# Attention's rows turned by VectorE's block transposes, and first weights in chunks of 128 rows

## The chip, the cores and the metric

The kernel runs on one core of one Trainium2 chip. The metric is the device time of one execution in microseconds (us). Before the change the median of 3 runs is 735.78 us (733.7 to 738.65).

## What is computed

Attention with two branches, then a layer of eight experts, of which each token takes one:

```python
# q, k, v: [8 batches, 8 heads, 576, 64] f32, about 0.1 x normal
q_d, k_d, v_d = means over each 4 tokens               # 144 tokens
out_up = repeat(softmax(q_d k_d^T / 8) v_d, 4)
scores = where(|i - j| < 4, q k^T / 8, -1e9)           # a band of 7 keys
attn_out = out_up + softmax(scores) v
x = attn_out.transpose(0, 2, 1, 3).reshape(4608, 512)  # column = 64 * head + d
logits = x @ w_gate + modality_bias[modality_id]       # w_gate [512, 8]
e = argmax(logits); gate = softmax(logits)[e]
out = gate * (relu(x @ w1[e]) @ w2[e])                 # w1 [8, 512, 1024], w2 [8, 1024, 512], all f32
```

## The kernel before

**Attention** works in 32 steps n, one for two heads of one batch (`b, hp = divmod(n, 4)`). A step loads q and k (L235) and v (L255) with SP's DMAs, turns q and k on TensorE (`tpq`, `tpk`, L279), copies them out of PSUM (`qT` on ScalarE, L299; `kT` on VectorE, L307), makes the band's scores (`sc`, L342), their maximum and exponentials, and turns the exponentials with VectorE's 32x32 block transposes (`lt`, L407). ScalarE spreads them into `Pw` (four copies, L412), and TensorE multiplies them with v (`avl`, L447). The branch of means goes through `scd` (L369), `de` (L382, L400), `pdt` (L418), `PdT` (L425) and `avd` (L432). VectorE adds both branches into X (L458). For a batch, X is `[128, 4, tokens]`: partition 64 a + d, second index 2 f + g, for the head 4 f + 2 a + g and its element d. GpSimd makes the sums over four (L313, L317) and two multiplications (L396, L400).

**Rows.** Each batch gives 4 or 5 tiles of 128 tokens, 36 in all. Per tile, `xr` turns X by four 128x128 transposes on TensorE into PSUM (L585; PSUM tag "T", of which there are three buffers, which q, k, the sums of v and `pdt` use too), `R` copies that on ScalarE into a row tile in the order of the reference's columns (L592), and `store` writes 128 rows of 2 KB to `xs` in HBM by one DMA of SP (L598). NR = 7 row tiles serve the first seven batches, four the last one.

**Routing.** Logits, the choice of expert and the places in a table are worked out for each batch (L494 to L575), and GpSimd scatters each token's number and gate into the table (L603). After four batches two units of 512 tokens are formed from the 2304 early rows; GpSimd fetches their table entries (L833) and gathers their rows from `xs` (L843).

**Experts.** 11 units follow: two early ones, six more of 512 tokens, one of 256, one of 128, one of 256. A unit needs an expert's weights in eight chunks of 512 KB: four of w1 (L792) and four of w2 (L795). A chunk lands in one of four `raw` buffers, ScalarE casts it to `hi` (L814) and VectorE subtracts for `lo` (L820); for the first four chunks GpSimd does part of that. There are 12 hi/lo buffers, used in turn; `step()` asks for a chunk four times in the first layer and four times in the second, eight chunks ahead. The gathered rows are turned on TensorE (L864) and split in the same way (L867, L869). Each product is three matmuls (hi x hi, hi x lo, lo x hi). A chunk of w1 holds all 512 rows and 256 of the 1024 columns, so `compute` needs chunk c for the output groups 2c and 2c+1 alone (L889). ReLU on ScalarE (L893) and VectorE (L894) gives the hidden values; the second layer (L937) goes to `o` (L940) and is scattered to the output by GpSimd (L941). The unit of 128 tokens (`compute_half`) has weights as the moving side, 256 columns at a time.

**Order.** Within Attention every instruction of every engine has a fixed place: `PHASE` gives each kind a due time in steps, `build` collects all calls, sorts them by `4 b + phase` or `n + phase`, and issues them in this order, so that each engine's queue is in the order of due times. SP's queue is one queue: the stores stand between the loads of q, k and v and, from the 28th step on, the first weights; a store that waits for its rows holds what is behind it. The last batch's routing and rows and the experts are ordered by a scheduler with priorities when the kernel is built.

Of the kernel before, what the change touches and what calls it, by code (L numbers as in the profile page):

```python
# [25 lines left out]
PAD = 3  # L26
# [19 lines left out]
NR = 7  # L46
# [33 lines left out]
class Consts:  # L80
# [48 lines left out]
    def load(s, tc, pool, work, rows, mid, bias, w_gate):  # L129
# [7 lines left out]
        s.mi = rows.tile([128, DM], F32, name="R", bufs=NR)[:36, :256].bitcast(I32)  # L137
# [41 lines left out]
    def biases(s, tc, pool, work, rows, psum):  # L179
# [11 lines left out]
        t1 = rows.tile([128, DM], F32, name="R", bufs=NR)[:, : 36 * NE].rearrange("p (t e) -> p t e", e=NE)  # L191
# [6 lines left out]
class Attention:  # L198
# [102 lines left out]
    def kT_(s, n, i):  # L301
# [4 lines left out]
        else:  # L306
            s.nc.vector.tensor_copy(s.kT2[:, g, PAD + 64 * g : PAD + 64 * g + 512], s.t.pop(("tp", "k", n)))  # L307
# [156 lines left out]
class Router:  # L464
# [116 lines left out]
    def xr(s, b, t):  # L581
        if t < s.t["G", b]:
            p = s.t["xr", b, t] = s.ps.tile([128, DM], F32, name="xr", tag="T", bufs=TB)
            for j in range(4):
                s.nc.tensor.transpose(p[:, 128 * j : 128 * j + 128], s.t["X", b][:, j, 128 * t : 128 * t + 128],  # L585
                                      s.C.ident)

    def R(s, b, t):

        if t < s.t["G", b]:  # L590
            R = s.t["R", b, t] = s.rp.tile([128, DM], F32, name="R", bufs=s.nr)
            s.nc.scalar.copy(R.rearrange("p (f a g d) -> p f g a d", f=2, a=2, g=2),  # L592
                             s.t.pop(("xr", b, t)).rearrange("p (f g a d) -> p f g a d", f=2, a=2, g=2))

    def store(s, b, t):
        if t < s.t["G", b]:
            r0 = 128 * (s.t["t0", b] + t)
            s.nc.sync.dma_start(s.xs[r0 : r0 + 128, :], s.t.pop(("R", b, t)))  # L598

# [625 lines left out]
```

## Time and profile before

| | us |
|---|---|
| median of 3 runs | 735.78 |
| the profiled execution's own time | 736.62 |
| its span, first to last instruction | 734.9 |
| Attention, up to the last `avl` matmul | about 288 |
| first expert matmul | 286.8 |
| last scatter to the output | 727.0 |

Times in the profile are us from the span's start. PE is TensorE's matmuls, PEld its weight loads, DVE VectorE, ACT ScalarE, POOL GpSimd, SP the engine that issues the plain DMAs. A line of a stage is `from:to length,` and then each engine's busy time with its count of instructions, the mean granted clock of TensorE, the mean busy share of 16 DMA engines, and GB/s. A group's line is: line, engine, operation, `out<-in`, shapes, count, then busy us, mean ns of one, idle time of the engine before it and what ended that. A wait's line is: who waited, for whom, total us, times, longest. A line of the timeline is start, length, engine, line, operation, count. "issue" is time in which an engine waited for nothing that the profile shows. Matmuls of TensorE overlap, so that a mean duration is longer than the distance between two.

### The profile page before, as it was taken

The numbers are of one execution on the slowest core, as the hardware profiler recorded it, in microseconds if no ns is written. First come the engines' busy times: TensorE is split into PE (matmuls) and PEld (weight loads), VectorE is DVE, ScalarE is ACT, GpSimd is POOL, SyncE is SP. The second block draws the span as 40 slices with busy tenths as digits, with TensorE's granted clock in tenths as the row PEclk, the third lists the DMA queues.
The fourth block names the chain that finished last, engine by engine and source line by source line (L and its number), as shares of the span: only waits on it lengthen the run. The fifth ranks groups of instructions, "written<-read, shape, count | busy, mean of one in ns | idle before, by whom it ended". The sixth has DMA issues, their size and how long they took to land. (4 is left out here: it accounts for less than half of the span.)

```text
span 734.9 us, 18972 instructions
## 1 busy us (share of the span) xinstructions
PE 682.7 (93%) x7635; PEld 555.0 (76%) x7635; DVE 379.5 (52%) x873; ACT 361.6 (49%) x808; POOL 298.7 (41%) x390
## 2 busy tenths in 40 slices
PE   6899898999968888997999999999999999999995
PEld 4678676777756766884888888888888888889894
DVE  4788575779745766650834424344243443326520
ACT  3578676777745766630434333343332433326620
POOL 6746564747757838266313243131412102211101
PEclk9899999999989999997999999999999999999998
DMA  9799999896786524944626235262452523526500
GB/s 180 154 192 176 184 187 182 159 211 119 172 156 195 86 85 113 278 146 154 200 74 217 86 118 194 82 219 72 143 172 96 191 85 99 175 87 211 180 13 28
DMA packets 175963, 107.89 MB, mean 147 GB/s; under 512 B 132765, under 2 KB 155329, under 8 KB 175874
## 3 DMA queue, kind: packets, MB, share of 16 engines
q1 hardware_dynamic: 167618, 87.44, 48.9%
q0 software_dynamic: 8256, 19.22, 7.9%
q8 instruction: 61, 1.00, 0.7%
q14 instruction: 28, 0.23, 0.1%
HBM read 87.39 MB, written 19.51 MB: 145 GB/s over the span
## 5 line engine op out<-in xcount | busy, mean ns | idle before, releaser
L820 DVE TENSOR_TENSOR wlo<-raw,whi 128x1024 fp32r<-128x1024 f32 x72 | 89.5, 1251 | 135.6 <-ACT whi L814 133.2
L941 POOL DMA_INDIRECT out_dram<-o,tg x37 | 39.6, 1070 | 253.6 <-ACT o L940 208.1
L814 ACT CAST whi<-raw 128x1024 fp32r<-128x1024 f32 x70 | 73.1, 1052 | 64.1 <-PE l L889 41.4
L937 PE MATMUL l<-whi,hh 128*128 128x512 f32 x256 | 100.5, 397 | 1.8 <-issue 1.7
L937 PE MATMUL l<-whi,hl 128*128 128x512 f32 x256 | 99.8, 392 | 1.1 <-issue 0.9
L937 PE MATMUL l<-wlo,hh 128*128 128x512 f32 x256 | 99.6, 391 | 1.1 <-issue 1.1
L889 PE MATMUL l<-xh,whi 128*128 128x512 f32 (+1 forms) x256 | 96.5, 379 | 0.6 <-issue 0.6
L889 PE MATMUL l<-xl,whi 128*128 128x512 f32 (+1 forms) x256 | 95.9, 375 | 0.8 <-issue 0.8
L889 PE MATMUL l<-xh,wlo 128*128 128x512 f32 (+1 forms) x256 | 96.0, 375 | 0.0
L940 ACT ACTIVATE o<-l,tg 128x512 f32<-128x512 f32 x37 | 25.4, 687 | 120.9 <-PE l L937 66.1
L893 ACT ACTIVATE hh<-l 128x512 fp32r<-128x512 f32 x72 | 42.8, 595 | 77.7 <-PE l L889 77.7
L894 DVE SCALAR_TENSOR_TENSOR hl<-l,hh 128x512 fp32r<-128x512 f32 x72 | 49.4, 688 | 59.8 <-ACT hh L893 59.8
L412 ACT COPY Pw<-lt 32x288 f32<-32x288 f32 x128 | 54.5, 426 | 7.8 <-DVE lt L407 6.1
L937 PEld LDWEIGHTS l<-whi,hl 128*128 128x128 f32 x256 | 48.2, 188 | 11.8 <-issue 2.5
L937 PEld LDWEIGHTS l<-wlo,hh 128*128 128x128 f32 x256 | 48.2, 188 | 11.6 <-issue 1.7
L937 PEld LDWEIGHTS l<-whi,hh 128*128 128x128 f32 x256 | 48.1, 188 | 11.3 <-issue 1.8
L889 PEld LDWEIGHTS l<-xl,whi 128*128 128x128 f32 x256 | 49.0, 191 | 9.8 <-issue 1.6
L889 PEld LDWEIGHTS l<-xh,whi 128*128 128x128 f32 x256 | 48.8, 191 | 9.6 <-issue 1.4
L889 PEld LDWEIGHTS l<-xh,wlo 128*128 128x128 f32 x256 | 48.8, 191 | 8.7 <-issue 0.4
L342 PE MATMUL sc<-kT,qT 64*24 64x32 f32 x3072 | 43.3, 193 | 10.9 <-issue 10.1
L603 POOL DMA_INDIRECT tab<-ig,si x36 | 39.1, 1086 | 34.4 <-DVE pn L720 12.2
L342 PEld LDWEIGHTS sc<-kT,qT 64*24 64x24 f32 x3072 | 33.7, 100 | 24.6 <-issue 20.2
(247 smaller groups left out, 1349.1 us busy)
## 6 DMA issues: line engine op xcount, KB each, us to landing
raw<-in_moe_w_dram SPq DMA_DIRECT2D x88, 512.0 KB
vw<-in_v_dram SPq DMA_DIRECT2D x53, 192.0 KB
xs<-R SPq DMA_DIRECT2D x36, 256.0 KB
qt<-in_q_dram SPq DMA_DIRECT2D x30, 288.0 KB
kt<-in_k_dram SPq DMA_DIRECT2D x30, 288.0 KB
vw<-in_v_dram SPq DMA_DIRECT2D x15, 96.0 KB
xg<-xs,tg POOLq DMA_INDIRECT x37
out_dram<-o,tg POOLq DMA_INDIRECT x37
```

The costliest lines, as they stand in the source:

```text
L342: s.nc.tensor.matmul(p[32 * j : 32 * j + SUB, i, :], qT[r, q0 : q0 + SUB], kT[r, q0 : q0 + WIN], start=False, stop=(i == NB - 1), skip_gro ...
L412: s.nc.scalar.copy(s.Pw[n % NPW][r, :, j, :SUB], s.t["lt", n][r, :, :SUB])
L603: i = nc.gpsimd.indirect_dma_start(out=s.tab[:, :], out_offset=bass.IndirectOffsetOnAxis(ap=C.si[:, t : t + 1], axis=0), in_=C.ig[:, t, :] ...
L814: (nc.gpsimd.tensor_copy if turn <= 4 else nc.scalar.copy)(hi, raw)
L820: (nc.gpsimd if 2 < turn <= 4 else nc.vector).tensor_tensor(lo, raw, hi.bitcast(F32), op=ALU.subtract)
L889: nc.tensor.matmul(p[:, 0 if H == 4 else f, :], a[:, k, fs], x[:, k, :N], start=(k == 0 and i == 0), stop=(k == 3 and i == 2))
L893: nc.scalar.activation(hh[:, g, :N], p, AF.Relu)
L894: nc.vector.scalar_tensor_tensor(hl[:, g, :N], p, 0.0, hh[:, g, :N].bitcast(F32), op0=ALU.max, op1=ALU.subtract)
L937: nc.tensor.matmul(p, a[:, f, hs], x[:, f % 2, :], start=(f == 0 and i == 0), stop=(f == 7 and i == 2))
L940: nc.scalar.mul(o, p, T[:, h, 1:2].bitcast(F32))
L941: nc.gpsimd.indirect_dma_start(out=s.out[:, :], out_offset=bass.IndirectOffsetOnAxis(ap=T[:, h, 0:1], axis=0), in_=o, in_offset=None, boun ...
```

## The change

1. `xr` and its PSUM tiles go. `R` is now a 32x32 block transpose on VectorE from X straight into the row tile. It turns each 32x32 block (32 partitions by 32 tokens), so a token's 512 values lie in four partition groups, in each as 4 x 32 values in a row. Two token tiles share a row tile of 4 KB a partition; NR = 4 of these serve the first batches, two the last one.
2. `store` writes two token tiles at a time (one, for the fifth of a batch) with four DMAs, one for each partition group, in pieces of 512 bytes. `xs` then has its 512 columns in another order: 16 groups of 32 values, sorted by partition group first.
3. So w1's rows are wanted in that order. A chunk of w1 is now 128 rows by all 1024 columns, loaded by four DMAs of 32 rows each (4 KB a row), and chunk k belongs to the k-th 128 values of a row. Every output group needs all four chunks. `compute` runs over output groups and then chunks; for the first unit, two output groups take chunks 0 and 1 and then chunks 2 and 3. `compute_half` multiplies 512 columns at a time.
4. `kT` is copied by ScalarE instead of VectorE, at another due time; R's due times stand where kT's had been within a step. The stores of a batch have three due times instead of five.

```diff
-NR = 7
+NR = 4
...
-    "tpq": 0.0000, "tpk": 0.0000, "qT0": 0.0000, "mk0": 0.0000, "tpt": 0.1888, "kT0": 0.2990, "qT1": 0.5097,
+    "tpq": 0.0000, "tpk": 0.0000, "qT0": 0.0000, "mk0": 0.0000, "tpt": 0.1888, "kT0": 0.2050, "qT1": 0.5097,
...
-    "X1": 3.6644, "X0": 3.6875, "xr0": 6.8416, "R0": 6.9346, "lg0": 7.0091, "lg1": 7.0155, "LT0": 7.1923,
-    "LT1": 7.2383, "xr3": 7.3162, "lgt0": 7.4172, "lgt1": 7.4353, "L1": 7.4440, "L0": 7.4639, "ch1": 7.4930,
-    "R3": 7.5485, "ch2": 7.5607, "ex": 7.6629, "gt": 7.8318, "pr": 7.8428, "xr4": 7.8664, "pl": 7.9316, "R4": 7.9883,
-    "xr1": 8.0166, "st4": 8.0780, "W0": 8.1749, "W3": 8.2403, "R1": 8.3185, "W4": 8.5513, "st2": 8.5946,
-    "st0": 8.7485, "xr2": 9.1244, "st3": 9.5946, "R2": 9.6525, "W1": 9.9527, "st1": 10.2000, "W2": 10.9537,
+    "X1": 3.6644, "X0": 3.6875, "lg0": 7.0091, "lg1": 7.0155, "LT0": 7.1923, "LT1": 7.2383, "R0": 7.2990,
+    "lgt0": 7.4172, "lgt1": 7.4353, "L1": 7.4440, "L0": 7.4639, "ch1": 7.4930, "ch2": 7.5607, "ex": 7.6629,
+    "R4": 7.7000, "gt": 7.8318, "pr": 7.8428, "pl": 7.9316, "st4": 8.0780, "W2": 8.1749, "R1": 8.2990, "W0": 8.5513,
+    "st2": 8.5946, "st0": 8.7485, "R2": 9.2990, "st3": 9.5946, "st1": 10.2000, "R3": 10.2990, "W1": 10.5513,
...
-            s.nc.vector.tensor_copy(s.kT2[:, g, PAD + 64 * g : PAD + 64 * g + 512], s.t.pop(("tp", "k", n)))
+            s.nc.scalar.copy(s.kT2[:, g, PAD + 64 * g : PAD + 64 * g + 512], s.t.pop(("tp", "k", n)))
...
-    def xr(s, b, t):
-        if t < s.t["G", b]:
-            p = s.t["xr", b, t] = s.ps.tile([128, DM], F32, name="xr", tag="T", bufs=TB)
-            for j in range(4):
-                s.nc.tensor.transpose(p[:, 128 * j : 128 * j + 128], s.t["X", b][:, j, 128 * t : 128 * t + 128],
-                                      s.C.ident)
-
     def R(s, b, t):
         if t < s.t["G", b]:
-            R = s.t["R", b, t] = s.rp.tile([128, DM], F32, name="R", bufs=s.nr)
-            s.nc.scalar.copy(R.rearrange("p (f a g d) -> p f g a d", f=2, a=2, g=2),
-                             s.t.pop(("xr", b, t)).rearrange("p (f g a d) -> p f g a d", f=2, a=2, g=2))
+            if t % 2 == 0:
+                one = t == 4 and b == B - 1
+                s.t["R", b, t // 2] = (s.rp.tile([128, 4, 4, 32], F32, name="o", bufs=3) if one else
+                                       s.rp.tile([128, 8, 4, 32], F32, name="R", bufs=s.nr))
+            R = s.t["R", b, t // 2][:, 4 * (t % 2) : 4 * (t % 2) + 4]
+            s.nc.vector.transpose(R, s.t["X", b][:, :, 128 * t : 128 * t + 128].rearrange("p k (i j) -> p i k j", j=32))
 
     def store(s, b, t):
-        if t < s.t["G", b]:
-            r0 = 128 * (s.t["t0", b] + t)
-            s.nc.sync.dma_start(s.xs[r0 : r0 + 128, :], s.t.pop(("R", b, t)))
+        n = min(2, s.t["G", b] - 2 * t)
+        if n > 0:
+            r0 = 128 * (s.t["t0", b] + 2 * t)
+            R = s.t.pop(("R", b, t))
+            for a in range(4):
+                s.nc.sync.dma_start(s.xs[r0 : r0 + 128 * n, 128 * a : 128 * a + 128].rearrange("(i j) x -> j i x", j=32),
+                                    R[32 * a : 32 * a + 32, : 4 * n].rearrange("p i k c -> p i (k c)"))
...
-            nc.sync.dma_start(raw.rearrange("p (k f) -> p k f", k=4),
-                              s.w1[bass.ds(e, 1), :, 256 * c : 256 * c + 256].rearrange("o (k p) f -> p (o k) f", p=128))
+            for i in range(4):
+                r = 256 * (i // 2) + 64 * (i % 2) + 128 * (c // 2) + 32 * (c % 2)
+                nc.sync.dma_start(raw[32 * i : 32 * i + 32], s.w1[bass.ds(e, 1), r : r + 32, :].rearrange("o p f -> (o p) f"))
...
+        early = H == 4 and s.turn["h"] == 0
+        for f, ks in [(f + j, k) for f in range(0, 8, 2) for k in ((0, 1), (2, 3)) for j in range(2)] if early else [
+                (f, range(4)) for f in range(8)]:
...
+            p, fs = ps[f // n], slice(128 * f, 128 * f + 128)
+            for k in ks:
+                wh, wl = W[k]
+                for i, (a, x) in enumerate(((wh, xh), (wh, xl), (wl, xh))):
+                    nc.tensor.matmul(p[:, f % n, :], a[:, fs], x[:, k, :N], start=(k == 0 and i == 0),
+                                     stop=(k == 3 and i == 2))
...
-            p = s.ps.tile([128, 2, 256], F32, name="l1", tag="S", bufs=SB)
-            for c in range(2):
-                step()
-                wh, wl = W[2 * g + c]
-                for k in range(4):
-                    for i, (a, x) in enumerate(((xh, wh), (xl, wh), (xh, wl))):
-                        nc.tensor.matmul(p[:, c, :], a[:, k, 0:128], x[:, k, :], start=(k == 0 and i == 0),
-                                         stop=(k == 3 and i == 2))
+            p = s.ps.tile([128, 512], F32, name="l1", tag="S", bufs=SB)
+            for k in range(4):
+                if k % 2 == 0:
+                    step()
+                wh, wl = W[k]
+                for i, (a, x) in enumerate(((xh, wh), (xl, wh), (xh, wl))):
+                    nc.tensor.matmul(p, a[:, k, 0:128], x[:, 512 * g : 512 * g + 512], start=(k == 0 and i == 0),
+                                     stop=(k == 3 and i == 2))
...
-            ro.rp, ro.nr = moe.xp, 4
+            ro.rp, ro.nr = moe.xp, 2
...
             for i in range(5):
-                ro.xr(b, i)
                 ro.R(b, i)
-                ro.store(b, i)
+                if i in (1, 3, 4):
+                    ro.store(b, i // 2)
```

More of the change, by code (lines that the diff above doesn't have):

```diff
@@ L136, in load @@
                                   w_gate[256 * f + 128 * a : 256 * f + 128 * a + 128].rearrange("(g d) e -> d g e", g=2))
-        s.mi = rows.tile([128, DM], F32, name="R", bufs=NR)[:36, :256].bitcast(I32)
+        s.mi = rows.tile([128, 2 * DM], F32, name="R", bufs=NR)[:36, :256].bitcast(I32)
         nc.sync.dma_start(s.mi, mid.bitcast(I32).rearrange("(t x) -> t x", t=36))
@@ L190, in biases @@
         s.tb = pool.tile([128, 36, NE], F32, name="tb")
-        t1 = rows.tile([128, DM], F32, name="R", bufs=NR)[:, : 36 * NE].rearrange("p (t e) -> p t e", e=NE)
+        t1 = rows.tile([128, 2 * DM], F32, name="R", bufs=NR)[:, : 36 * NE].rearrange("p (t e) -> p t e", e=NE)
         for dst, mm, r in ((s.tb, m0, 0), (t1, m1, 1)):
@@ L821, in wsplit @@
         if which == 0:
[L822 removed]
+            return hi, lo
         return hi.rearrange("p (f d) -> p f d", f=2), lo.rearrange("p (f d) -> p f d", f=2)
```

33 lines of the change are left out of this document (13 added, 20 removed).

## The prediction

> **What bounds the kernel now.** I read the page's head first, then busy time by stage, then groups of instructions, waits, and short stretches of the timeline. The page:
>
> ```profile
> span 734.9 us, 18972 instructions
> PE 682.7 (93%) x7635; PEld 555.0 (76%) x7635; DVE 379.5 (52%) x873; ACT 361.6 (49%) x808; POOL 298.7 (41%) x390
> ```
>
> TensorE is busy for 93% of the span, but that is a mean. By stage (busy us of each engine, clock, DMA share, GB/s):
>
> ```profile
> core 0: us, PE busy (x) PEld busy (x) DVE busy (x) ACT busy (x) POOL busy (x), PEclk, DMA share, GB/s
> 30.00:210.00 180.00, 168.32 (x3943) 133.40 (x3939) 133.93 (x417) 131.90 (x402) 114.35 (x164) 0.99 0.91 173
> 210.00:287.00 77.00, 59.73 (x1176) 47.95 (x1173) 46.68 (x133) 47.73 (x138) 50.44 (x63) 0.91 0.53 127
> 287.00:337.00 50.00, 50.00 (x261) 39.65 (x261) 28.07 (x79) 21.16 (x32) 27.41 (x24) 1.00 0.65 200
> 337.00:348.00 11.00, 5.62 (x12) 2.70 (x12) 0.00 (x0) 0.49 (x1) 5.99 (x6) 0.71 0.41 120
> 348.00:660.00 312.00, 312.00 (x1425) 258.50 (x1424) 126.68 (x162) 119.67 (x166) 73.94 (x70) 0.99 0.42 136
> 660.00:726.00 66.00, 64.85 (x401) 57.88 (x399) 27.59 (x29) 28.32 (x37) 6.20 (x6) 1.00 0.36 117
> ```
>
> Attention runs to 287 us. To 210 us TensorE is busy 168.3 of 180 us (94%), VectorE 74%, ScalarE 73%, and the DMA engines 91%: TensorE is the bound and DMA stands close behind. From 210 to 287 us TensorE has 17 us of holes. From 287 us the experts bind TensorE without a hole, but for 337 to 348 us. So work taken from TensorE is worth most of itself where its row is full, about half of itself from 210 to 287 us, and work given to VectorE or ScalarE is free unless their queues begin to bind.
>
> **What leaves TensorE.** The groups, and the transposes of Attention's rows by stage:
>
> ```profile
> L585 PE MATMUL xr<-ident,X 128*128 128x128 f32 x144 | 23.5, 289 | 0.1
> L592 ACT COPY R<-xr 128x512 f32<-128x512 f32 x36 | 20.8, 584 | 3.9 <-PE xr L585 3.6
> L307 DVE COPY kT<-tp 128x512 f32<-128x512 f32 x32 | 21.1, 658 | 10.1 <-PE tp L279 10.0
> L407 DVE STREAM_TRANSPOSE lt<-le 128x384 f32<-128x384 f32 x32 | 18.2, 569 | 8.9 <-POOL le L396 8.9
> L458 DVE TENSOR_TENSOR X<-avl,Od 128x288 f32<-128x288 f32 x48 | 20.3, 447 | 1.0 <-PE avl L447 0.8
> L458 DVE TENSOR_TENSOR X<-avl,Od 128x224 f32<-128x224 f32 x16 | 6.1, 380 | 0.2
> L299 ACT ACTIVATE qT<-tp 128x512 f32<-128x512 f32 x32 | 19.2, 600 | 10.7 <-PE tp L279 9.2 <-issue 0.6 <-ACT R L592 0.4
> 30.00:210.00 180.00, 13.77 (x88) 9.69 (x88) 12.84 (x22) 0.99 0.91 173
> 210.00:287.00 77.00, 6.92 (x36) 5.14 (x36) 5.26 (x9) 0.91 0.53 127
> 287.00:337.00 50.00, 2.83 (x20) 2.40 (x20) 2.71 (x5) 1.00 0.65 200
> ```
>
> 144 transposes are 36 tiles of four: 22 tiles to 210 us, 9 to 287 us, 5 among the first expert's matmuls. The busy time overstates them, since matmuls overlap. What a tile holds up is the distance to what starts next, in the timeline:
>
> ```profile
> 135.47 0.60 PE L279 MATMUL tp<-ident,qt 128*128 128x128 f32 x4
> 135.91 0.60 PE L279 MATMUL tp<-ident,kt 128*128 128x128 f32 x4
> 136.34 0.25 PE L333 MATMUL sc<-mask,identb 128*128 128x192 bf16 x1
> 136.43 0.60 PE L585 MATMUL xr<-ident,X 128*128 128x128 f32 x4
> 136.96 0.60 PE L342 MATMUL sc<-kT,qT 64*24 64x32 f32 x48
> ```
>
> Four transposes of this shape take 0.44 us (135.47 to 135.91). So 36 tiles give 15.8 us at most, as long as nothing else holds the end. That isn't all had:
>
> - The last 5 tiles stand between the first expert's matmuls, where TensorE has no hole: 5 x 0.44 = 2.2 us, all of it.
> - The 22 tiles before 210 us: 22 x 0.44 = 9.7 us. Here the other engines are near. One short step (of two heads) of the stage:
>
> ```profile
> 135.00:141.00 6.00, 6.00 (x163) 5.21 (x161) 5.12 (x14) 5.42 (x18) 5.56 (x9) 1.00 0.66 130
> ```
>
> ScalarE is busy 5.42 of 6.00 us, GpSimd 5.56. Such a step can shrink by 0.44 us, but only if every queue is entered without loss. I take 80%: 7.7 us. Bounds: 0, if ScalarE or GpSimd hold each step, and 9.7.
> - The 9 tiles of 210 to 287 us: 4.0 us, of which I take half, 2.0 us, since TensorE waits there for others a fifth of the time. Bounds 0 and 4.0.
>
> Together 11.9 us, bounds 2.2 and 15.8.
>
> **What VectorE and ScalarE get.** The new block transpose of 128x512 is not in the trace; its nearest row is the same operation on 128x384, 569 ns. By the two rows of L458, 64 elements more cost 67 ns, so 128 more cost 134 ns and the new one about 0.70 us. It reads X in four strided pieces; bounds are 0.57 us, and 1.14 us (two of the 384-wide). 36 of them are 25.3 us (20.5 to 41.0). VectorE gives up the 32 kT copies, 32 x 0.658 = 21.1 us, whose place in each step the transposes take. Net +4.2 us on an engine with 46 us idle before 210 us: 0. The Trainium skill, "VectorE: DVE Perf Modes", section "The three transpose paths", gives 311 ns for a 128x128 VectorE transpose in bf16; an estimate from that page is 4 x 311 = 1.24 us a tile, VectorE would gain 24 us of work and the sum would stay, with more weight on the second rival below. The row of 569 ns for three such blocks speaks against it.
>
> ScalarE loses 36 R copies, 21.0 us, and gets 32 kT copies from PSUM, priced as qT's at 600 ns: 19.2 us. Net -1.8 us: 0. But they move: the kT copy stands between qT and the three Pw copies for which TensorE's avl matmuls wait. Third rival.
>
> **Stores and queues.** SP's waits and issues (name of the issue: least, median, most ns), and the stretches that price a packet:
>
> ```profile
> SPq L795 <- DVE wlo L820: 158.9, 33, 19.3
> SPq L598 <- ACT R L592: 35.2, 12, 10.5
> SPq L235 <- PE tp L279: 15.0, 5, 6.4
> PE vp L267 <- DMA vw<-in_v_dram: 3.8, 2, 3.4
> L598 SPq DMA_DIRECT2D xs<-R x36: 319/584/3671, 76.1 to 311.2; - x36
> L792 SPq DMA_DIRECT2D raw<-in_moe_w_dram x44: 316/373/440, 229.9 to 679.9; - x44
> 30.00:60.00 30.00, 28.74 (x735) 23.10 (x732) 23.38 (x72) 22.88 (x74) 18.35 (x28) 1.00 0.92 181
> 327.00:331.00 4.00, 4.00 (x21) 3.27 (x21) 0.69 (x1) 1.16 (x2) 3.08 (x4) 1.00 0.90 311
> 690.00:695.00 5.00, 5.00 (x44) 4.92 (x42) 3.50 (x3) 3.50 (x5) 1.01 (x1) 1.00 0.93 309
> ```
>
> From 30 to 60 us nearly all is 256-byte loads of q, k and v: 181 GB/s at a share of 0.92 of 16 engines is 12.3 bytes per ns and engine, 21 ns a packet. From 327 to 331 us it is 1-KB pieces of the first weights: 21.6 bytes per ns, 47 ns. From 690 to 695 us it is mostly 2-KB pieces of the second: 20.8, so 99 ns. A 512-byte piece lies between 21 and 47 ns; on the line between them 30 ns. The stores are now 4608 packets of 2 KB, 28 us of 16 engines; they become 18432 of 512 bytes, 34 us (24 to 54). Over 230 us that is +6 us of DMA work. Loads of q, k and v have hidden nearly always: TensorE's largest wait for one is 3.8 us in all. SP itself waits 15.0 us for TensorE to free load buffers, so the loads run ahead. I take 0; without that cover it costs the 6 us.
>
> SP issues 80 store DMAs for 36, 44 more at 0.32 to 0.58 us: 14 to 26 us of SP; and four for one on 44 weight chunks, 132 more at 0.32 to 0.37 us: 42 to 49 us of SP over 490 us. SP waits 158.9 us for VectorE to free weight buffers on one line alone, so the weights have room. Behind a store that waits for R stand the loads of q, k and v; SP now waits at three places in a batch instead of four or five. 0.
>
> **First layer's order.** It does the same matmuls, but the first of a unit's eight output groups needs all four chunks. For the first unit the chunks are needed in pairs. Timeline of GpSimd and TensorE there:
>
> ```profile
> 288.37 2.38 POOL L820 TENSOR_TENSOR wlo<-raw,whi 128x1024 fp32r<-128x1024 f32 x1
> 286.78 0.96 PE L889 MATMUL l<-xh,whi 128*128 128x512 f32 x3
> 705.00:710.00 5.00, 5.00 (x44) 5.00 (x43) 0.69 (x1) 1.11 (x2) 0.97 (x1) 1.00 0.12 48
> ```
>
> The fourth chunk's low part ends at 290.75 us; it is wanted by the 18th matmul after 286.78 us, and with 0.22 us for one (312.0 us over 1425 from 348 to 660 us) that is 290.5 us. So 0 to 0.5 us; I take 0. The unit of one block has 24 matmuls of 512 columns for 48 of 256: 24 x 0.22 = 5.3 us for 48 x 0.114 (5.00 us over 44) = 5.5 us. 0.
>
> **The sum.** 7.7 + 2.0 + 2.2 = 11.9 us less. The profiled run's own time is 736.6 us, 1.7 us above its span and 0.8 above the median of the runs shown: 736.6 - 11.9 = 724.7, which for the median is 723.9. I say 724. 1% is 7.4 us, about what a measurement tells from no change.
>
> **Rivals.**
>
> 1. *The hole at 337 to 348 us goes too.* TensorE does 12 matmuls there in 11 us, and the clock falls to 0.71; VectorE and ScalarE stand still, and the releaser named is "issue", so no data is late. In attention the same name stands for
>
> ```profile
> PEld sc L342 <- issue: 20.2, 52, 2.3
> PE sc L342 <- issue: 10.1, 17, 2.2
> ```
>
> The change takes 288 instructions from TensorE's stream and shifts all behind them, so this hole may move or vanish: 12 matmuls need 2.7 us, so up to 8.3 us more, 716. Against it: nothing in the change aims there, and an equal hole may open elsewhere. The Trainium skill, "Runtime: NRT & Kernel Launch", section "Instruction fetch mechanics", holds that instructions come in blocks while the last block runs, mostly hidden; if so the hole isn't a matter of fetching and stays. The rows of 20.2 and 10.1 us fit that rule badly, if fetching is what "issue" hides; they don't name it. Chance 0.12.
> 2. *The queues become the bound.* ScalarE and GpSimd, at 90% and 93% in a short step, hold the steps where they are, and only the last 5 tiles and a fifth of the others count: 2.2 + 0.2 x 13.7 = 4.9 us less, 731. The transposes of VectorE don't matter here. For it: 5.42 and 5.56 of 6.00 us. Against: the steps with v's sums last 7 us and longer, and leave room. Chance 0.22.
> 3. *Slower: ScalarE's order.* The kT copy delays each step's Pw copies by 0.60 us, and avl stands in TensorE's order behind them. If TensorE waits it out in each of 32 steps, that is 19.2 us against 15.8 saved: +3.4, 740. It decides when the third Pw copy ends after the end of scd. Against it: the R copies that go lie in the same queue, after or between the Pw copies, and are 21.0 us. Chance 0.09.
> 4. *Much slower: all four chunks at once.* If at a unit's start three more splits must end first (1.25 us each by the row below), nine of the units behind the first lose 9 x 3.75 = 34 us: 736.6 - 11.9 + 34 = 759, 758 for the median.
>
> ```profile
> L820 DVE TENSOR_TENSOR wlo<-raw,whi 128x1024 fp32r<-128x1024 f32 x72 | 89.5, 1251 | 135.6 <-ACT whi L814 133.2
> ```
>
> It decides when the last first-layer split ends behind the unit's first matmul. Against it: 312.0 of 312.0 us busy over six unit borders, and SP's 158.9 us of waiting because buffers are still full. Chance 0.07, the ends of the list where less is loaded ahead included.
>
> **How the numbers follow.** The forecast, 724, has 0.50; its own range is 718 to 730. The range that holds 8 in 10 takes in the missing hole at 716 and the slower ScalarE at 740: 714 to 741. Faster by over 1% (below 728.4): the first rival's 0.12 and 0.46 of the forecast's 0.50, 0.58 in all. Within 1%: the forecast's other 0.04, the second rival's 0.22 and 0.05 of the third, 0.31. Slower: the fourth's 0.07 and 0.04 of the third, 0.11.
>
> **What would show it.** L585 is gone; VectorE has 36 transposes of about 0.70 us in the line R; TensorE's first matmul of L889's successor starts near 277 us for 286.8, and its end stands 12 us earlier. TensorE stays over 93% busy from 30 to 200 us. Wrong: waits "avl <- ACT kT" or "avl <- ACT Pw" of over 5 us (third), waits for first weights at a unit's start (fourth), TensorE waits for loads of over 10 us (DMA), or an expert stage that is not as long as before.

## The result and the profile after

The changed kernel takes 732.42 us (median of 20 runs, 725.63 to 737.82), the kernel before beside it 736.34 us (median of 20, 733.09 to 743.65). The ratio is 0.9933, with an interval of 0.9905 to 0.9961: 4 us faster, where 12 were forecast. A ratio leaves out executions that lie more than 1.5% above a kernel's fastest, so it can differ by half a per cent from the quotient of the medians, which are of all runs.

The profiled execution took 737.82 us, 5 us over its median, and its span is no shorter than the one before. The head of its page, with the busy time of each engine:

```profile
span 735.8 us, 19186 instructions
PE 670.7 (91%) x7467; PEld 540.8 (73%) x7467; DVE 381.1 (52%) x877; ACT 358.3 (49%) x804; POOL 296.9 (40%) x390
```

TensorE is busy 12.0 us less (670.7 for 682.7). The forecast had up to 15.8 us of work leave TensorE and 11.9 us leave the span, so that the 12.0 looks like the forecast's number is chance. This execution's span shows none of it. The same stages as before the change (busy us of each engine, clock, DMA share, GB/s):

```profile
30.00:210.00 180.00, 161.59 (x3895) 126.96 (x3892) 132.93 (x414) 132.58 (x404) 113.89 (x164) 0.99 0.89 170
210.00:287.00 77.00, 60.65 (x1077) 46.31 (x1078) 53.36 (x143) 46.59 (x132) 54.06 (x64) 0.87 0.68 133
287.00:337.00 50.00, 47.56 (x230) 37.12 (x229) 26.18 (x78) 16.47 (x25) 22.61 (x22) 1.00 0.72 197
337.00:348.00 11.00, 2.71 (x6) 1.34 (x5) 0.00 (x0) 0.69 (x1) 7.85 (x8) 0.66 0.51 145
348.00:660.00 312.00, 310.83 (x1417) 257.16 (x1417) 126.39 (x162) 119.27 (x165) 71.04 (x69) 0.99 0.45 135
660.00:726.00 66.00, 64.46 (x377) 56.84 (x376) 27.50 (x29) 28.08 (x37) 6.54 (x6) 1.00 0.39 121
```

To 210 us TensorE is busy 161.59 us for 168.32. The hole at 337 us is still there, and the stretch before it is no longer full. The groups for the moved work:

```profile
L588 DVE STREAM_TRANSPOSE R<-X 128x512 f32<-128x512 f32 x35 | 23.5, 677 | 0.3 <-DMA vw<-in_v_dram 0.3
L306 ACT COPY kT<-tp 128x512 f32<-128x512 f32 x32 | 18.7, 585 | 2.9 <-PE tp L278 2.6
```

Both cost what was forecast (0.70 and 0.60 us). Last, TensorE's waits: on the experts' first layer, on the scores, and on GpSimd's de:

```profile
PE sc L341 <- issue: 16.3, 21, 2.9
PE l L892 <- issue: 9.5, 7, 1.7
PE pdt L417 <- POOL de L399: 11.4, 7, 5.2
```

Before, the wait on the scores was 10.1 us, and the others were these (the second layer, L937, is where the first trace of before had most of its hole):

```profile
PE pdt L418 <- POOL de L400: 9.2, 4, 6.2
PE l L937 <- issue: 3.7, 3, 1.7
PE l L889 <- issue: 1.4, 2, 0.8
```

So the execution gained in attention (its first expert matmul starts at 282.91 us for 286.78) and lost that at the second expert unit.

One trace of each isn't enough here, since the slowest execution of a kernel lies 1 to 3% above its fastest. What follows therefore splits each trace in three, by the start of a unit's first matmul from xh in the timeline: attention (to the first unit), units 1 to 3, and the rest of the span. Three starts, of the changed kernel, of a second trace of it (a_third) and of a second trace of the kernel before (b_again):

```profile
282.91 0.96 PE L892 MATMUL l<-xh,whi 128*128 128x512 f32 x3
```
```profile
269.77 0.96 PE L892 MATMUL l<-xh,whi 128*128 128x512 f32 x3
```
```profile
280.03 0.96 PE L889 MATMUL l<-xh,whi 128*128 128x512 f32 x3
```

| kernel | attention | units 1-3 | rest | profiled run | median | before's median beside it |
|---|---|---|---|---|---|---|
| before, first trace | 286.8 | 153.9 | 294.2 | 736.6 | 735.8 | |
| b_again | 280.0 | 145.0 | 294.8 | 721.6 | 721.6 | 723.4 |
| changed, first trace | 282.9 | 158.2 | 294.7 | 737.8 | 732.4 | 736.3 |
| a_again | 274.1 | 155.8 | 294.7 | 726.6 | 727.2 | 733.6 |
| a_third | 269.8 | 154.4 | 294.8 | 721.0 | 729.0 | 732.6 |
| b_noxr | 282.2 | 148.0 | 293.7 | 725.6 | 724.0 | 733.6 |
| b_kTact | 276.5 | 145.0 | 294.1 | 717.4 | 720.4 | 723.4 |
| b_chunks | 287.5 | 161.9 | 294.3 | 745.5 | 741.3 | 732.6 |
| b_st512 | 286.1 | 155.0 | 293.8 | 736.7 | 734.4 | 732.6 |
| a_oldchunks | 272.3 | 162.9 | 300.3 | 737.2 | 736.2 | 732.6 |
| b_spread | 282.6 | 151.6 | 294.3 | 730.3 | 728.1 | 733.6 |
| a_spread | 271.4 | 158.2 | 295.1 | 726.4 | 734.5 | 733.6 |
| b_spread2 | 278.7 | 142.9 | 299.2 | 722.6 | 723.1 | 723.4 |
| a_spread2 | 268.7 | 151.4 | 302.0 | 724.2 | 727.7 | 723.4 |
| a_late2 | 277.5 | 154.8 | 294.3 | 728.4 | 729.1 | 732.7 |
| b_s3l2 | 287.7 | 142.8 | 299.9 | 732.6 | 726.6 | 732.7 |
| b_chunks_s3l2 | 286.2 | 143.2 | 302.1 | 733.3 | 732.6 | 732.7 |
| a_spread3late2 | 277.5 | 145.2 | 301.8 | 726.4 | 722.3 | 732.7 |
| b_best5 | 288.2 | 142.8 | 296.2 | 729.2 | 723.1 | 734.0 |
| a_best5 | 277.3 | 145.2 | 297.3 | 721.6 | 719.7 | 734.0 |

Names with b_ are variants of the kernel before, with a_ of the changed one. Only kernels of one group are compared in time: the kernel before itself had medians from 723.4 to 736.3 us in six groups. Each split is of one execution, and the last digit is good to 0.1 us. A later full unit takes 45.4 us, with TensorE busy throughout.

### The profile page after: what moved, and what is told of

It reads as the page before. It is cut to its first block, busy times and chain, and to the rows that moved or that the text cites. A ratio compares the mean times of both kernels' runs of the same rounds, so it can differ in the third digit from the quotient of the medians.

```text
span 735.8 us, 19186 instructions
## 1 busy us (share of the span) xinstructions
PE 670.7 (91%) x7467; PEld 540.8 (73%) x7467; DVE 381.1 (52%) x877; ACT 358.3 (49%) x804; POOL 296.9 (40%) x390
## 5 line engine op out<-in xcount | busy, mean ns | idle before, releaser
L821 DVE TENSOR_TENSOR wlo<-raw,whi 128x1024 fp32r<-128x1024 f32 x72 | 86.8, 1234 | 92.8 <-ACT whi L815 89.1
L815 ACT CAST whi<-raw 128x1024 fp32r<-128x1024 f32 x70 | 70.7, 1050 | 30.1 <-issue 12.0
L943 ACT ACTIVATE o<-l,tg 128x512 f32<-128x512 f32 x37 | 25.4, 687 | 110.4 <-PE l L940 58.2
L341 PE MATMUL sc<-kT,qT 64*24 64x32 f32 x3072 | 45.4, 194 | 16.9 <-issue 16.3
```

The source lines that it names most:

```text
L341: s.nc.tensor.matmul(p[32 * j : 32 * j + SUB, i, :], qT[r, q0 : q0 + SUB], kT[r, q0 : q0 + WIN], start=False, stop=(i == NB - 1), skip_gro ...
L815: (nc.gpsimd.tensor_copy if turn <= 4 else nc.scalar.copy)(hi, raw)
L821: (nc.gpsimd if 2 < turn <= 4 else nc.vector).tensor_tensor(lo, raw, hi.bitcast(F32), op=ALU.subtract)
L943: nc.scalar.mul(o, p, T[:, h, 1:2].bitcast(F32))
```

## The experiments

**First group: is the gain given back, or did the new parts cost it?** The changed kernel again:

> The changed kernel again, unaltered, timed beside the kernels of this group. Both theories: 4 to 6 us faster than before (ratio 0.992 to 0.995). Theory 1 (TensorE did shed 12 us, and what is missing is given back at places whose time GpSimd's chain of indirect DMAs sets): the first expert matmul 4 us earlier than in before, and a hole in TensorE's work at 337 to 350 us that lies at the same time as in before. Theory 2 (the new parts, that is kT on ScalarE, the chunk order and the 512-byte stores, cost 6 to 7 us): TensorE's waits on kT, on stores or on weights are longer than in before by that much.

727.17 us against 733.56, ratio 0.9979 (0.9939 to 1.0019): 6.4 us by the medians and 0.2% by the ratio, so neither lies where it was expected. Attention ended 12.7 us earlier than in the first trace of before, and units 1 to 3 took 155.8 us. The loss behind attention was there again, at another absolute time: the second unit began at 324.3 us and its hole lay at 324.8 to 337.7. So "at the same time as in before", which both traces of the change's first comparison had shown, was chance.

The next two move one gather. In the edit below, moe.hold makes the gather wait for the last output scatter:

```diff
-            gather(i + 2)
+            if i != 1:
+                gather(i + 2)
...
+                def mid(h):
+                    split(i + 1, h)
+                    if i == 1 and h == 1:
+                        moe.hold = moe.lastout
+                        gather(3)
...
```

> The kernel before, with the fourth unit's gather of entries and rows (eight indirect DMAs) moved from the start of the second unit to after the first scatter in that unit's second layer, so that GpSimd's unbroken row of indirect DMAs at 310 to 345 us is shorter by eight of 1.3 us. Theory 1, with the hole at 337 to 348 us put down to that row: the hole shrinks from 8 us of idle and slow clock to under 2, and the kernel is 7 to 10 us faster (726 to 729 us). Rival: the hole comes from something else at that place (the change of stage, the weights, the second layer's own inputs): hole and time unchanged, 735 to 738 us.

728.14 us, ratio 0.9897 (0.9821 to 0.9973): faster, but only 5 us by the medians, where 7 to 10 were expected.

> The changed kernel with the same move of the fourth unit's gather. Theory 1: the hole is gone and the 4 us that attention won reach the end: 722 to 725 us, 12 to 14 us faster than before. Rival as for the same move in the kernel before: 731 to 734 us, no more than the change alone.

734.5 us, ratio 1.0024 (0.9979 to 1.0069): nothing gained, a miss. The hole was not gone from either; it had moved with the row of indirect DMAs. TensorE's waits from 370 to 400 us in a_spread, and the first and the last gather of the joined row on GpSimd there:

```profile
PE l L892 <- issue: 5.7, 5, 1.7
```
```profile
360.57 0.99 POOL L834 DMA_INDIRECT tg<-tab,pidx  x1 [0.30 <-issue]
...
382.64 1.46 POOL L844 DMA_INDIRECT xg<-xs,tg  x1 [0.30 <-issue]
```

This hole lay at 376.5 to 386 us, at the start of the third unit (373.3 us), and the second unit's was gone. The moved gather stood directly ahead of the next one in GpSimd's queue.

The last of the group takes the transposes off TensorE; ScalarE copies X unturned from where it lies, and nothing else changes:

```diff
     def xr(s, b, t):
-        if t < s.t["G", b]:
...
+        pass
...
-            s.nc.scalar.copy(R.rearrange("p (f a g d) -> p f g a d", f=2, a=2, g=2), s.t.pop(("xr", b, t))...)
+            s.nc.scalar.copy(R.rearrange("p (k j) -> p k j", k=4), s.t["X", b][:, :, 128 * t : 128 * t + 128])
```

> The kernel before without the 36 groups of four transposes on TensorE: ScalarE copies the unturned block of X into the stored tile, so the rows that are stored, and the output, are not turned; kT, the weight chunks, the stores and the order of everything else are those of before. Theory 1: shedding TensorE's work alone gives what the whole change gives, 4 to 6 us (730 to 732 us), with the hole at the same time. Theory 2: it gives the full 11 to 12 us (724 to 725 us), and the new parts took 6 to 7 us of them back.

723.97 us against 733.56, ratio 0.9889 (0.9831 to 0.9947): 9.6 us by the medians, where the whole change gave 6.4 beside it. That spoke for theory 2: TensorE's work is worth nearly what was forecast, and the change pays part of it back somewhere. The trace makes this less sure. Its attention is only 4.6 us shorter than in the first trace of before and 2.2 us longer than in the second (b_again, below), and it has no hole: units 1 to 3 took 148.0 us. So part of the 9.6 us can be the missing hole.

**Second group: the hole, and kT.**

> The kernel before, unaltered, as one of the kernels of this group: it shows how far two sets of executions of one kernel lie apart, and gives a second trace of it. Ratio within 0.995 to 1.005. Theory 1: the second trace also has a hole of 8 to 14 us at TensorE between 320 and 350 us, beginning 12 to 16 us after the start of GpSimd's unbroken row of indirect DMAs and ending within 3 us of its end; and the first expert matmul at 280 to 290 us. Rival (the hole belongs to the first trace alone): none.

721.58 us, ratio 0.999 (0.9946 to 1.0033). The trace refuted theory 1 as it stood. GpSimd's row of indirect DMAs ran from 315.45 to 339 us, as in the first trace, and TensorE had no hole from 290 to 400 us; its only wait there was

```profile
PE l L889 <- DVE hl L894: 1.1, 1, 1.1
```

So a long row on GpSimd doesn't always bring the hole.

> The changed kernel with every later gather (units 3 on) issued after the first scatter of the unit two before it, so that no two gathers stand back to back in GpSimd's queue; when the fourth unit's gather alone was moved, it ran into the fifth's and the hole moved with the joined row to 376 us. Theory 1 (the hole is a row of more than some 12 indirect DMAs on GpSimd): no hole over 3 us from 287 us on, third unit's start at 366 to 370 us, and 712 to 718 us, 10 to 14 us under the changed kernel. Rival (the hole belongs to the start of a unit whose weights or rows have just come): a hole again, and 725 to 730 us.

727.68 us, ratio 1.0105 (1.0042 to 1.0168): slower, a miss, though the hole was gone. Units 1 to 3 still took 151.4 us, now with a wait that has a name:

```profile
PE l L892 <- DVE hl L897: 6.8, 1, 6.8
```

and the rest of the span was 7 us longer.

> The kernel before with the same spreading of its gathers. Theory 1: no hole over 3 us from 287 us on, 8 to 12 us faster than before (ratio 0.984 to 0.989). With the changed kernel so spread still 10 to 12 us faster than this one, since then nothing takes TensorE's relief back. Rival: ratio 0.995 to 1.005.

723.09 us, ratio 1.0018 (0.9974 to 1.0062): a miss too. Units 1 to 3 took 142.9 us, and the rest gave back 4 to 5.

```diff
-    "kT0": 0.2990,
+    "kT0": 0.2050,
-            s.nc.vector.tensor_copy(s.kT2[:, g, ...], s.t.pop(("tp", "k", n)))
+            s.nc.scalar.copy(s.kT2[:, g, ...], s.t.pop(("tp", "k", n)))
```

> The kernel before with kT's 32 evictions on ScalarE (0.59 us each there, 18.7 us in all) in place of VectorE and at the changed kernel's place in the order; ScalarE still evicts the 36 turned tiles too, so it carries 19 us more than before and VectorE 21 us less. Theory 1 (kT's place costs nothing): within 2 us of before (ratio 0.997 to 1.003). Theory 2 (kT ahead of the weights Pw on ScalarE holds up TensorE): 3 to 8 us slower, with the wait of avl on Pw or of sc on kT grown to 3 us and over.

720.38 us, ratio 1.0027 (0.9992 to 1.0062): kT on ScalarE costs nothing that can be measured, even with the 36 evictions still there.

**Third group: the chunks and the stores.**

> The changed kernel unaltered, beside the kernels of this group and the kernel before on the same chip in the same stretch of time. The second trace of before had no hole between 290 and 400 us (TensorE's unexplained waits there 0 us, against 6.8 in the first) and was 17 us shorter, with the same row of indirect DMAs on GpSimd; so the hole comes and goes between sets of executions, and theory 1's tie to GpSimd's row alone has fallen. Theory 3 (what attention gains is lost in the first two expert units, because the 128-row chunks of w1 are all needed at a unit's start and all freed only at the end of its first layer): first expert matmul at 268 to 275 us whatever the hole does, second unit 6 to 14 us longer than the 45.4 us of the later units, and the whole 0 to 5 us under before. Rival (no such tie): second unit under 49 us where the hole is absent, and 9 to 12 us under before.

729.04 us against 732.64, ratio 0.9971 (0.9931 to 1.001). Attention at 269.8 us, second unit 58.0 us. Theory 3 had said both, though what the trace shows in the second unit is the hole. TensorE from 320 us on, where the second unit begins, by stretches and in its timeline:

```profile
320.00:335.00 15.00, 5.91 (x17) 3.68 (x16) 1.10 (x1) 2.82 (x4) 8.85 (x9) 0.71 0.52 148
335.00:378.00 43.00, 43.00 (x197) 35.44 (x196) 24.24 (x47) 18.06 (x25) 12.98 (x12) 0.98 0.48 143
```
```profile
321.25 0.39 PE L892 MATMUL l<-xh,wlo 128*128 128x512 f32 x1
321.85 0.40 PE L892 MATMUL l<-xh,whl 128*128 128x512 f32 x1 [0.21 <-issue]
323.94 0.39 PE L892 MATMUL l<-xl,whl 128*128 128x512 f32 x1 [1.70 <-issue]
326.08 0.53 PE L892 MATMUL l<-xh,whl 128*128 128x512 f32 x1 [1.75 <-issue]
```

Seventeen matmuls in 15 us, with no releaser named where it waits, and then 197 without a gap. The row on GpSimd, 19 indirect DMAs with no pause of 0.9 us between two of them, begins and ends so:

```profile
306.92 0.99 POOL L834 DMA_INDIRECT tg<-tab,pidx  x1 [3.39 <-DVE xl L870]
...
330.27 1.03 POOL L944 DMA_INDIRECT out_dram<-o,tg  x1 [0.30 <-issue]
```

All four traces with the changed kernel's own chunks and gathers (the fourth is a_late2 below) have this hole within 3 us of the second unit's start.

The old chunks put back into the changed kernel; the order of the stored columns makes one chunk eight DMAs:

```diff
-            for i in range(4):
-                r = 256 * (i // 2) + 64 * (i % 2) + 128 * (c // 2) + 32 * (c % 2)
-                nc.sync.dma_start(raw[32 * i : 32 * i + 32], s.w1[bass.ds(e, 1), r : r + 32, :]...)
+            for i in range(4):
+                r, g = 256 * (i // 2), 64 * (i % 2)
+                for b in range(2):
+                    nc.sync.dma_start(raw[32 * i : 32 * i + 32].rearrange("j (a b f) -> j a b f", a=2, b=2)[:, :, b], ...)
```

> The changed kernel with the old chunks of w1 (256 columns of all rows; in the changed order of the rows this takes eight DMAs of 1-KB pieces a chunk) and the old order of the first layer's matmuls; VectorE's transposes, kT on ScalarE and the 512-byte stores stay. Theory 3: the second unit is 45 to 49 us long and the kernel is 5 to 9 us faster than the changed one. Rival (the chunks cost nothing): within 2 us of the changed one, or slower by what the eight DMAs cost SyncE.

736.16 us, ratio 1.0079 (1.0033 to 1.0124), 7 us over the changed kernel. TensorE now waited in the first unit too (4.8 us for hh), and the rest of the span grew by 5.5 us (300.3 for 294.8); that the eight DMAs a chunk cost this is likely, not shown. So the time decides nothing on the chunks. The trace does decide one thing: with the old chunks back, the second unit still took 59.4 us and had the hole, where theory 3 wanted 45 to 49. So the hole comes without the new chunks too.

The chunks alone, in the kernel before, with rows in natural order and the changed kernel's order of the first layer's matmuls:

```diff
-            nc.sync.dma_start(raw.rearrange("p (k f) -> p k f", k=4), s.w1[bass.ds(e, 1), :, 256 * c : 256 * c + 256]...)
+            for i in range(4):
+                r = 128 * c + 32 * i
+                nc.sync.dma_start(raw[32 * i : 32 * i + 32], s.w1[bass.ds(e, 1), r : r + 32, :]...)
...
```

> The kernel before with the 128-row chunks of w1 in four DMAs each and the changed order of the first layer's matmuls (rows in natural order), nothing else changed. Theory 3: second unit 6 to 14 us longer than 45.4, and the kernel 4 to 8 us slower than before (ratio 1.005 to 1.011). Rival: ratio 0.997 to 1.003.

741.27 us against 732.64, ratio 1.0121 (1.0045 to 1.0196): 8.6 us slower by the medians. The second unit took 63.8 us, and here there is no "issue" but a chain of names. TensorE's waits from 287 to 440 us:

```profile
PE l L892 <- DVE hl L897: 8.6, 1, 8.6
PE l L892 <- ACT o L943: 4.9, 1, 4.9
```

What ScalarE, VectorE and GpSimd do there, in their timelines:

```profile
349.53 0.69 ACT L943 ACTIVATE o<-l,tg 128x512 f32<-128x512 f32 x1 [8.99 <-DMA out_dram<-o,tg]
```
```profile
356.52 0.43 DVE L638 TENSOR_TENSOR o<-ltri,mn 128x256 f32<-128x256 f32 x1 [16.07 <-DMA out_dram<-o,tg]
```
```profile
345.39 0.94 POOL L834 DMA_INDIRECT tg<-tab,pidx  x1 [0.30 <-issue]
346.64 1.02 POOL L944 DMA_INDIRECT out_dram<-o,tg  x1 [0.30 <-issue]
```

ScalarE's next output tile and VectorE's table at L638 (for the late lists; it borrows the same three buffers o) both wait for the first unit's scatters to land. Those stand on GpSimd behind the gathers: here the first scatter is issued at 346.64 us, after twelve indirect DMAs of two gathers that began at 329.01. In b_again, with the old chunks, only five stood ahead of it:

```profile
320.50 1.02 POOL L843 DMA_INDIRECT xg<-xs,tg  x1 [0.31 <-issue]
321.82 1.02 POOL L941 DMA_INDIRECT out_dram<-o,tg  x1 [0.31 <-issue]
...
339.31 0.42 DVE L638 TENSOR_TENSOR o<-ltri,mn 128x256 f32<-128x256 f32 x1 [5.14 <-DMA out_dram<-o,tg]
```

This order isn't written out in the kernel's text: gathers and scatters stand in the same lines in both kernels, and yet their places on GpSimd differ.

```diff
-            s.nc.sync.dma_start(s.xs[r0 : r0 + 128, :], s.t.pop(("R", b, t)))
+            R = s.t.pop(("R", b, t))
+            for a in range(4):
+                s.nc.sync.dma_start(s.xs[r0 : r0 + 128, 128 * a : 128 * a + 128], R[:, 128 * a : 128 * a + 128])
```

> The kernel before with each of its 36 stores of rows made as four DMAs in pieces of 512 bytes (144 DMAs on SyncE in place of 36; the changed kernel makes 76). Theory 3 and theory 1: the stores are off the path, ratio 0.997 to 1.004. Theory 2 (the small pieces fill the DMA engines in attention, where they are 83 to 97% busy): 3 to 6 us slower, with the waits on kt, qt and vw grown.

734.39 us, ratio 1.0016 (0.9968 to 1.0064): no cost that can be measured, with 144 store DMAs where the changed kernel has 80. Its trace, of a kernel with the old chunks, has the hole too: the second unit took 57.0 us.

**Fourth group: does mending GpSimd's order give the forecast's time?** The tables moved by one unit:

```diff
-            if i == 1:
+            if i == 2:
                 lists["m"] = ro.late(cnt, moe.xp)
```

> The changed kernel with the tables of the late lists (the 24 small VectorE instructions of lines 638 to 752, which write into the three buffers o that the output tiles use) made in the third unit in place of the second. Theory 3a (the second unit's loss is VectorE standing at these tables for a buffer o that unit 1's scatters, queued behind the gathers on GpSimd, hold, with hl behind it): waits on hl at the start of the second unit gone, second unit 46 to 49 us where no hole of unexplained waits lies in it, 722 to 726 us if before is 733. Theory 3b (the loss is in the chunks themselves: weights and slots): second unit 52 to 60 us, 728 to 731 us.

729.11 us against 732.67, ratio 0.9972 (0.9934 to 1.0009), second unit 58.2 us with the hole (9.3 us of "issue"). The tables alone are not the loss.

In the next three the tables are moved, and all gathers, the third unit's too, come after a scatter (the condition in mid is h == 1 alone).

> The changed kernel with the late tables moved as in the run beside it, and with every gather issued after the first scatter of the unit two before it, the third unit's gather too: the first unit's scatters no longer stand behind eleven indirect DMAs. Theory 3a: units two and three 45 to 49 us each, no unexplained hole, 10 to 13 us under before (720 to 723 if before is 733). Theory 3b: second unit 52 us and more, 3 to 5 us under before.

722.34 us, ratio 0.9886 (0.9832 to 0.994), units 1 to 3 in 145.2 us: theory 3a's time and units.

> The kernel before with the 128-row chunks (1.2% slower by themselves, 9 us) and with the same two moves of gathers and late tables. Theory 3a: the 9 us are gone, ratio 0.990 to 1.001, second unit 45 to 49 us. Theory 3b: still 6 to 9 us slower than before, ratio 1.008 to 1.013.

732.56 us, ratio 1.0054 (1.0008 to 1.0101). The units were as theory 3a had them, 52.0, 45.7 and 45.5 us, with TensorE full in each:

```profile
286.20:338.20 52.00, 52.00 (x272) 41.26 (x269) 31.27 (x82) 24.93 (x38) 26.64 (x21) 1.00 0.76 183
338.20:383.90 45.70, 45.70 (x210) 37.50 (x209) 16.00 (x19) 15.43 (x22) 14.72 (x15) 1.00 0.49 152
383.90:429.40 45.50, 45.50 (x210) 37.59 (x209) 22.40 (x45) 17.68 (x25) 11.93 (x11) 1.00 0.44 131
```

Its second scatter is issued at 333.62 us, ahead of the rows' gather. Yet the time was not quite theory 3a's: the medians are level with before (732.56 and 732.67), and the ratio lies between 3a's 1.001 and 3b's 1.008. The moves alone are the measure for it:

> The kernel before with the two moves of gathers and late tables alone, as the measure for the run of the chunks beside it and of what the moves give without the change. All theories: 0 to 6 us faster than before (ratio 0.991 to 1.000), more where the unexplained hole at 337 to 350 us is present in before.

726.6 us, ratio 0.9932 (0.9895 to 0.9969). So with nothing lost in units 1 to 3, the chunks still cost 6 us by the medians (732.56 against 726.6; 5.1 by the means, and 1.2% by the two ratios).

**Last: the moves without their own loss.** The short units' gathers stay in place (gather(i + 2) in mid for i up to 5, at the unit's start after that).

> The changed kernel with late tables and gathers moved as in the run before, but only for the full units: the short units' gathers stay where they were, since the moved ones left TensorE waiting 3.5 us at 680 us and made the stretch from the fourth unit on 7 us longer (302 us against 294). Theory 3a with this: that stretch 294 to 296 us, units two and three under 49 us, 14 to 18 us under before (715 to 719 if before is 733). Theory 3b: 6 to 10 us under before.

719.73 us against 733.98, ratio 0.9784 (0.973 to 0.9837), 14 us under before, as theory 3a had it, and the fastest version of the study.

> The kernel before with the same moves. Theory 3a (the change is worth its full 10 to 12 us once nothing in units two and three takes it back): 5 to 8 us under before, and 9 to 12 us over the changed kernel moved alike. Theory 3b (the chunks still cost some 6 us in it): 10 to 13 us under before, and 3 to 6 us over the changed kernel moved alike.

723.06 us, ratio 0.9848 (0.98 to 0.9895). The changed kernel is 3.3 us under it by the medians, 5.2 by the means (718.5 and 723.7, with standard errors of 1.4 each): both numbers are as theory 3b had them, and the 9 to 12 us between the two that 3a wanted are not there.

## Why the prediction was right or wrong

**Right: what the parts cost where they run.** VectorE's transposes took 0.677 us, kT on ScalarE 0.585 us. (The estimate of 1.24 us, four times what the Trainium skill's "VectorE: DVE Perf Modes", section "The three transpose paths", gives for a 128x128 bf16 transpose, was too high; the measurement decides against it for this shape.) kT's new place (1.0027) and the small stores (1.0016) cost nothing, as put down; no wait of TensorE on q, k or v grew past 4 us, and "avl <- ACT Pw" was 0.8 us in all (0.7 before). The third rival didn't happen.

**Right in its number, on the mean: attention.** The forecast put the first expert matmul near 277 us, 9.7 us earlier. The eight traces with the changed attention (a_oldchunks left out) have it at 268.7 to 282.9, mean 274.9. The six with the old attention and old chunks and stores (b_kTact left out) have it at 278.7 to 288.2, mean 284.0. The difference is 9.1 us, with a standard error of 2.4. In the first pair of traces it was 3.9, which alone would have misled. TensorE was then not over 93% busy to 200 us, as the forecast had it, but 90% to 210 us (161.59 of 180): the freed time didn't fill up again. That the 9.1 us come from TensorE's shed work, as the forecast has it, isn't shown: in single traces, which scatter by about 4 us, taking out the transposes alone (b_noxr) put the first expert matmul at 282.2 us, 1.8 under the mean of 284.0, and moving kT alone (b_kTact) at 276.5, 7.5 under it.

**Not refuted: the 11.9 us for what leaves TensorE.** Taking out the transposes alone gave 9.6 us by the medians (by the ratio 0.5 to 1.7%, 4 to 12 us). How much of this is the hole, which its trace doesn't have, is open.

**Wrong: "First layer's order", put at 0 to 0.5 us,** and with it the experts' stage taken to stay as long as before. This is the step that failed; an experts' stage "not as long as before" was one of the prediction's own signs of being wrong. The chunks alone cost 8.6 us in the kernel before (ratio 1.0121), and 6 us with the gathers moved. The step asked only whether the first unit's weights are there when its matmuls want them, and they are: the first unit takes 50 to 53 us in every trace of the changed kernel. What it didn't ask is which instructions of other engines are ordered by that work. In the one trace of the chunks alone GpSimd's first scatter came behind twelve indirect DMAs in place of five, ScalarE and VectorE waited for the scatters, and TensorE's second unit was 63.8 us long; with scatters ahead of the gathers it was 45.7. So that order explains the long second unit of this trace. It isn't shown to be what the 8.6 us are, since most of them stayed when the second unit was mended.

In the changed kernel units 1 to 3 cost 6.6 us more than in the kernel before (mean of three traces 156.1, of two 149.5), and what its traces show there is the second unit's hole. The 6.6 us are rough, since the two traces of before, one with a hole and one without, lie 8.9 us apart. Nor are they the chunks' in the way that b_chunks shows: b_chunks has no hole, and a_oldchunks and b_st512 have the hole with the old chunks. So two losses are on record, the chunks' cost (measured without the rest of the change) and the hole, and how they add up in the changed kernel isn't shown.

By the stages' means the change is then 9.1 us gained in attention less 6.6 lost in units 1 to 3, 2.5 us left, and the rest of the span alike within 1 us; measured in three groups were 3.6 to 6.4 us by the medians and 0.2 to 0.7% (1.5 to 5 us) by the ratios. With standard errors of 2.4 us for attention and 4.6 for the units this agrees, but not by more than the errors allow.

**The fourth rival, all four chunks at once,** had the right part of the change and the wrong mechanism and size: it had each later unit wait for splits, 34 us. The later borders stayed full, as its counterevidence had said (310.83 of 312.00 us); the one that broke lies ahead of that stretch.

**The first rival, the hole:** it neither went for good nor stayed. It is missing in one of two traces of the unaltered kernel before and present in all three of the changed one. Set beside the longest row of indirect DMAs on GpSimd from 300 to 400 us, counted in all twenty traces, it shows an order that the prediction had not looked for:

| longest row | traces | "issue" hole of TensorE |
|---|---|---|
| 19 | changed, a_again, a_third, a_late2, a_oldchunks, a_spread, b_spread, b_st512 | in all eight, 7 to 13 us long |
| 18 | before, b_again, b_kTact | in before alone |
| 14 | b_chunks, b_noxr | none; their waits (up to 8.6 and 2.1 us) have names |
| 11 and less | the seven with spread gathers | none over 1.4 us |

Each hole begins 14 to 20 us into its row and ends 1.9 to 2.8 us after it (a_third: row 306.9 to 331.3, hole 321.3 to 333.8). The kernel before stands at 18, where it came once in three; the changed kernel at 19, where it always came. That the length of the row is the cause is not shown by this: the spread gathers change the order of the scatters as well as the length.

**What stays open.** First, what stops TensorE beside a row of that length: what it waits for isn't in the profile, and no row of a length between 14 and 18 was tried. Fetching of its instructions has little for it: in a_third the 16-KiB packets of the instruction queue started at 316.4 and 356.1 us and none in the hole between, which agrees with the Trainium skill's "Runtime: NRT & Kernel Launch", section "Instruction fetch mechanics", that a block comes while the last one runs. In seven of the nine traces with a hole such a packet started 3.5 to 6.3 us ahead of it, but b_again had one at 325.8 us and no hole, so this is neither shown nor ruled out. Second, where the chunks' last 6 us lie. In the kernels with moved gathers units 1 to 3 are alike with and without chunks (143.2 and 142.8) and the rest differs by 2.2 us; the remainder would have to be in attention, where one trace scatters by 4 us and more. So why the change was worth about 4 us both before and after units 1 to 3 were mended, and not 10, is not known.

## What to carry to other kernels

A change that only reorders an engine's own work can reorder another engine's queue wherever the order is worked out by the program: after such a change, compare each in-order queue, the DMA-issuing one first, and look for results that now stand behind loads and hold buffers. Add up a gain by stages over several traces before explaining a single one, since one trace of this kernel was off by more than the whole effect. And a part of a change that is put down at nothing is best tried alone: it costs one run and found here what no row of the profile before had shown.

## What was not expected of the hardware

In its holes TensorE starts matmuls 1.4 or 2.1 us apart (a_third: 321.85, 323.94, 326.08 us, for 0.23 us outside), while GpSimd goes on issuing an indirect DMA every 1.3 us; VectorE and ScalarE do almost nothing with it (1.1 and 2.8 us of 15). The clock falls to 0.71 in that stretch, and just behind the hole matmuls are still 0.43 us apart (a_third: 334.18, 334.61 us), so a hole costs more than its idle time.

An output scatter took about 3 to 7 us from issue until the buffer that it reads was used again (b_chunks: issued at 346.64, ScalarE's next output tile at 349.53 us; b_again: issued at 332.61, VectorE's L638 at 339.31 us), against 1.0 us of GpSimd. Three buffers that look ample by GpSimd's busy time were not.
